# Softmax sums carried as logarithms in the attention of a fused transformer block, with other slots, and two modulation rows sent by way of DRAM

## The chip, the cores and the metric

The kernel runs on one core of a Trainium2 chip. The core has five engines with instruction streams of their own: PE (TensorE, the matrix engine), DVE (VectorE), ACT (ScalarE), POOL (GpSimd) and SP (SyncE, which here only issues transfers). They meet through semaphores alone. Every stream runs in order: an instruction that waits holds up all that stand behind it on its engine. The metric is the device time of one execution in microseconds (us); three runs gave 2748.44, 2750.02 and 2751.23 us, a median of 2750.02 us.

## The reference

One transformer block on 2048 tokens of width 1024, in float32. Six rows of length 1024 (`sa, ca, ga, sb, cb, gb`) come from a small product of a condition vector. Then a normalised and modulated input goes through attention with 32 heads of 32 columns, in four segments of 512 tokens. Inside a segment the softmax is causal; what came before the segment is read through a running sum, the memory:

```python
logits = jnp.einsum("bhqd,bhkd->bhqk", qs, ks) * scale + mask
p = _softmax(logits, axis=-1)
a_dot = jnp.einsum("bhqk,bhkd->bhqd", p, vs)
num = jnp.einsum("bhld,bhde->bhle", pq, M)
den = jnp.einsum("bhld,bhd->bhl", pq, z)[..., None] + 1e-6
a_mem = num / den
o = g * a_mem + (1.0 - g) * a_dot
M = M + jnp.einsum("bhld,bhle->bhde", pk, vs)
...
x = x + ga * _A_ref(h, ...)
h = _layernorm(x, axis=-1) * (1 + cb) + sb
x = x + gb * _B_ref(h, ...)
```

`g` is one number for each head (the sigmoid of `beta`); `_B_ref` is a gated feed-forward of width 3584.

## The kernel before

A factor of every large product is split into a high and a low float32r part, and three products (high·high, high·low, low·high) give the accuracy. The program has four stages: `start` (the six rows, the first segment), 33 steps of attention, the projection with `wo` and the second norm, and the feed-forward (gate and up, then down), which takes the last 1600 us or so.

**The steps of attention.** Step `n` has a group `g` of four heads and a segment `s` (list `steps`, line 1545: first half segments 0 and 1 by turns for each group, second half segments 2 and 3). The work of one (group, segment) is spread over three steps: the products for q, k and v of it are made in step `n-1` (parts K and Q), its scores S, sums A and memory M in step `n`, its values V in step `n+1`. The string `ORDER` (line 1546) is the order in which the parts take turns; each letter runs its generator to the next `yield`. PE's stream is exactly in this order. The streams of DVE, ACT, POOL and SP in this stage are ordered by a scheduler, which lays them out ahead of time by its own costs.

**Scores (S, line 678).** For each block `i` of 128 queries and each head `j`, PE makes a score tile in one of five PSUM banks (`s_ps`). DVE (line 691) adds the mask, copies the negated scores to `sj` and keeps the negated maximum in `mm`; ACT (line 693) takes the exponential of `sj` and keeps its sum in `ll`. When four blocks are done, DVE splits `mm` into a high and a low part `mt`, turns these with four 32x32 transposes into rows `tt` (line 704) and writes them with four `tensor_scalar`s into partitions 96 to 128 of `qs` (line 706). So the product `T` of the values part (line 753), which is the score tile turned round (keys as rows), comes out of PE with the maximum already taken off. Four such `T` products, one for each head, can run only when all four writes of `qs` are done.

**Values (V, line 740).** ACT takes the exponential of `T` into `pt` (line 755), POOL zeroes what the mask forbids (756), and PE multiplies with the values into `po` (762), whose rows are columns of heads and whose columns are queries. The inverse sums are needed in the same orientation: DVE makes `rc = (1-g)/ll` with `omg = 1-g` (710, 711), ACT spreads it to 128 columns `rx` (713), PE turns `rx` with four 128x128 transposes (776, tile `R`), ACT copies the result out (780), DVE multiplies `po` by it (781). For segments after the first, the memory's part `ry` is turned by PE in the same way (tile `Y`) and added by DVE (784).

**K and Q.** A quarter of v or k is six products of 128x512 on PE. The ninth turn of K (line 407) sends k to `ks` and turns it with four transposes (`kT`, line 362), which ACT (`ek`, 364) and DVE (365, 367) make into `pk` for the sums.

**Rows ga and gb.** The columns `modT` hold the six rows as columns. `row_parts` (line 120) makes a row on all partitions of it: DVE puts the columns on two diagonal matrices, PE multiplies them with ones (line 131), ACT copies (132). `gab` is used for `wo` (line 806), `gbb` in the down product.

**Second norm.** `norm_tiles(..., "b")` (line 208) goes through eight tiles of 128 tokens: SP loads a tile `nb` of `x1_d` (line 215) into one of two buffers, DVE takes the statistics, POOL the root, ACT scales it (206), PE turns it (228, `tpb`), ACT shifts it (233, `htb`), SP stores it.

## Time and profile before

| what | value |
|---|---|
| median of three runs | 2750.02 us |
| the profiled execution, its own time | 2750.67 us |
| its span on the core | 2748.8 us |
| busy: PE, DVE, ACT, POOL | 99%, 64%, 47%, 19% of the span |
| PE in the chain that ended last | 91% |

The span is the time from the first instruction of the program to the last; 1.9 us of the execution's own time lie around it. A busy PE row counts from the start of a matrix instruction to its modelled end; since the next one starts before that end, what an instruction takes from PE is read from start to start in the timeline. A wait list names, for each idle time of an engine, the engine whose instruction ended it.

### The profile page before, as it was taken

Reading aid. Unit: us, or ns where it says so; the run is one execution under the profiler, and the core shown is the slowest. Engines: PE = TensorE matmul, PEld = TensorE weight load, DVE = VectorE, ACT = ScalarE, POOL = GpSimd, SP = SyncE. Lnnn points to the kernel's source line nnn. Section 1 sums busy time; section 2 is a strip of 40 time slices with the busy share of each in tenths; the row PEclk is TensorE's granted clock in tenths of the full one; section 3 lists DMA queues with packets and bytes.
Section 4 is the critical chain, followed back from the end, with each engine's and each line's share of the span. In section 5 each row is a group of like instructions: output and inputs, shape, how many; then the busy total and the mean of one; then the engine's idle time right before and its main releaser. Section 6 shows DMA issues by size and latency. Waiting matters only on the chain.

```text
span 2748.8 us, 38576 instructions
## 1 busy us (share of the span) xinstructions
PE 2722.0 (99%) x13346; PEld 2206.8 (80%) x13346; DVE 1755.5 (64%) x3727; ACT 1290.6 (47%) x2858; POOL 515.9 (19%) x970
## 2 busy tenths in 40 slices
PE   8999999999999999999999999999999999999999
PEld 5777877777777777788888888888888888888887
DVE  7566657666666735777777777666777754434552
ACT  6788877677776735333433334223322243332220
POOL 1333333333333421100000000000000003013352
PEclk9999999999999999999999999999999999999999
DMA  8666655665554657656655656433566695544552
GB/s 260 131 139 155 151 116 120 160 140 123 122 114 92 170 187 233 212 209 216 211 210 176 230 205 227 150 123 146 204 249 244 221 311 178 168 140 164 199 193 81
DMA packets 229844, 486.47 MB, mean 177 GB/s; under 512 B 17552, under 2 KB 92560, under 8 KB 229648
## 3 DMA queue, kind: packets, MB, share of 16 engines
q1 hardware_dynamic: 227776, 477.58, 57.5%
q0 software_dynamic: 1728, 6.29, 0.6%
q8 instruction: 105, 1.72, 0.3%
q14 instruction: 91, 0.75, 0.1%
q10 hardware_dynamic: 144, 0.13, 0.0%
HBM read 304.11 MB, written 129.50 MB: 158 GB/s over the span
## 4 chain that ended last, share of the span: by engine, by line
PE 91%; DVE 3%; DMA 3%; ACT 2%; issue 1%; POOL 0%; SPq 0%; DVEq 0%; POOLq 0%; ACTq 0%
PE f L1338 38%; PE d L1509 19%; PE k L320 5%; PE y L821 5%; PE q L320 5%; PE v L320 5%; PE T L753 3%; PE S L689 3%; PE O L762 3%; PE M L669 1%; PE num L727 1%; PE R L776 1%; DMA r<-wv 1%; PE vT L336 1%; ACT sj L693 0%
## 5 line engine op out<-in xcount | busy, mean ns | idle before, releaser
L1338 PE MATMUL f<-A,B 128*128 128x512 f32 x4704 | 1071.8, 390 | 1.2 <-DVE c L1303 0.7
L1338 PEld LDWEIGHTS f<-A,B 128*128 128x128 f32 x4704 | 881.5, 188 | 184.9 <-DVE c L1303 1.1
L1509 PE MATMUL d<-wb,ah 128*128 128x512 f32 x2352 | 534.2, 389 | 0.1
L1509 PEld LDWEIGHTS d<-wb,ah 128*128 128x128 f32 x2352 | 441.5, 188 | 92.4 <-DVE wb L1389 0.5
L691 DVE CUSTOM_DVE_ANT_0 sj<-S,mask 128x384 f32<-128x384 f32 (+3 forms) x512 | 227.2, 487 | 138.3 <-PE S L689 125.3
L693 ACT ACTIVATE sj<-sj,mm 128x384 f32<-128x384 f32 (+3 forms) x512 | 282.1, 558 | 28.4 <-DVE mm L691 26.1
L755 ACT ACTIVATE pt<-T 128x256 f32<-128x256 f32 (+3 forms) x512 | 183.0, 446 | 118.1 <-PE T L753 116.5
L1389 DVE TENSOR_TENSOR ah<-ar,ah 128x1792 fp32r<-128x1792 f32 x56 | 116.2, 2075 | 169.3 <-ACT ah L1388 169.3
L1388 ACT ACTIVATE ah<-ar 128x1792 fp32r<-128x1792 f32 x56 | 95.4, 1703 | 273.8 <-PE d L1509 232.9
L756 POOL TENSOR_SCALAR_AFFINE_SELECT pt<-pt 128x128 f32<-128x128 f32 x512 | 151.4, 315 | 315.1 <-ACT pt L755 308.1
L162 POOL TENSOR_TENSOR w<-r,w 128x256 fp32r<-128x256 f32 x180 | 140.6, 812 | 179.2 <-ACT w L155 160.8
L1305 ACT ACTIVATE g<-g 128x512 f32<-128x512 f32 x56 | 35.4, 633 | 287.0 <-DVE g L1305 287.0
L955 DVE TENSOR_TENSOR B<-t,B 128x512 fp32r<-128x512 f32 x168 | 115.5, 688 | 57.6 <-ACT B L958 57.5
L1414 POOL TENSOR_TENSOR yo<-u,gbb 128x256 f32<-128x256 f32 x32 | 30.1, 972 | 557.2 <-ACT gbb L132 557.2
L958 ACT ACTIVATE B<-t 128x512 fp32r<-128x512 f32 x168 | 105.5, 628 | 58.3 <-PE f L1338 56.0
L821 PE MATMUL y<-wo,hho 128*128 128x512 f32 x384 | 125.9, 393 | 0.0
L1302 ACT ACTIVATE g<-f 128x512 f32<-128x512 f32 x56 | 33.6, 599 | 178.7 <-PE f L1338 178.6
L753 PEld LDWEIGHTS T<-qs,ks 128*128 128x128 f32 x512 | 83.2, 188 | 39.3 <-issue 21.5
L753 PE MATMUL T<-qs,ks 128*128 128x256 f32 (+2 forms) x512 | 111.7, 336 | 3.0 <-DVE ry L735 2.0
L689 PE MATMUL S<-ks,qs 96*128 96x256 f32 (+2 forms) x512 | 110.8, 335 | 2.0 <-DVE mm L691 1.8
L1432 POOL TENSOR_TENSOR xo<-xo,yo 128x256 f32<-128x256 f32 x64 | 71.1, 1141 | 211.8 <-DMA xo<-x_d 196.7
L955 DVE TENSOR_TENSOR B<-rg,B 128x512 fp32r<-128x512 f32 x112 | 77.2, 689 | 51.2 <-ACT B L958 51.1
(255 smaller groups left out, 4314.9 us busy)
## 6 DMA issues: line engine op xcount, KB each, us to landing
ar<-hid_d SPq DMA_DIRECT2D x56, 896.0 KB, 5.2
rg<-wg SPq DMA_DIRECT2D x56, 512.0 KB, 4.7
ru<-wu SPq DMA_DIRECT2D x56, 512.0 KB, 5.5
hid_d<-g SPq DMA_DIRECT2D x56, 512.0 KB, 3.1
sc<-hid_d SPq DMA_DIRECT2D x56, 512.0 KB, 5.7
hid_d<-sc SPq DMA_DIRECT2D x56, 512.0 KB, 2.9
br<-wT_d SPq DMA_DIRECT2D x49, 512.0 KB, 6.1
ks<-kh SPq DMA_DIRECT2D x64, 256.0 KB, 5.6
```

The source lines that it names most:

```text
L162: eng.tensor_sub(w[:, 1, k:k + 256], r[:, k:k + 256], f32(w[:, 0, k:k + 256]))
L320: nc.tensor.matmul(ps, w[:, a], b, start=(kt == 0 and a == 0 and b is hi), stop=(kt == KT - 1 and a == 1))
L689: nc.tensor.matmul(ps[:, :nk], qs[:96, j, i * P:(i + 1) * P], ks[:96, j, :nk], start=True, stop=True)
L691: nc.vector.tensor_tensor_reduce(out=sj[:, :nv], in0=ps[:, :nv], in1=mask[:, L - nv:], scale=-1.0, scalar=3.4e38, op0=ALU.add, op1=ALU.min ...
L693: nc.scalar.activation(sj[:, :nv], sj[:, :nv], AF.Exp, bias=mm[:, j, i:i + 1], scale=-1.0, accum_out=ll[:, i, j:j + 1])
L753: nc.tensor.matmul(ps[:, :nn], ks[:, j, kc * P:(kc + 1) * P], qs[:, j, L - nn:], start=True, stop=True)
L755: nc.scalar.activation(pt, ps[:, nn - n:nn], AF.Exp)
L756: nc.gpsimd.affine_select(pt[:, :P], pt[:, :P], pattern=[[1, P]], compare_op=ALU.is_ge, fill=0.0, base=0, channel_multiplier=-1)
L821: nc.tensor.matmul(ps, b[:, i * P:(i + 1) * P], w[:, a, g % 2], start=(g == 0 and a == 0 and b is hi), stop=(g == G - 1 and a == 1))
L955: eng.tensor_sub(dst[:, k], a[:, k], b[:, k])
L1338: nc.tensor.matmul(ps, B[m, i][:, a, kt * P:(kt + 1) * P], A[p, i, kt][b], start=(start and kt == 0 and a == 0 and b == 0), stop=(kt == 3 ...
L1509: nc.tensor.matmul(ps[t], ops[n][:, x, k, t * P:(t + 1) * P], b[:, y, kk % 2], start=(kk == 0 and x == 0 and y == 0), stop=(kk == 13 and x ...
```

## The change

`ll` becomes its logarithm on ACT and is taken off the (negated) maximum before this is split and turned. So the row that `qs` carries into `T` holds maximum and logarithm of the sum, and the exponential of `T` is the softmax itself. `rc`, `rx`, the four `R` transposes, their copy and the multiplication go; `omg` holds 1-g for each row of `po`, and one DVE instruction makes `po * omg + Y` from it, where `Y` is copied out of PSUM by ACT. Of the four writes of `qs`, those for `i` 1 and 3 go to ACT.

`ORDER` is another one, and the last step has its own (`LAST`, with the old places of T). The first part of V (the four `T` for the first block of keys) stands one turn of K later, the ninth turn of K (with `kT`) stands between the first and the second block of scores and no longer behind the fourth, and the `Y` part ends V. `ga` and `gb` are written to DRAM as columns and read back as a row on all partitions. The loads of `nb` in the second norm are issued by ACT in place of SP. The table of ACT's functions that is loaded at the start is named by the program; it holds both exponential and logarithm.

```diff
+    def row_out(q, c):
+        nc.sync.dma_start(row_d[q * KT:(q + 1) * KT].rearrange("k p -> p k"), modT[:, c:c + KT])
+    def row_in(dst, q):
+        nc.sync.dma_start(dst, row_d[q * KT:(q + 1) * KT].rearrange("k p -> (k p)").unsqueeze(0).to_broadcast([P, D]))
...
         def load(q):
             xs[q] = get(f"n{name}{toks[q]}")
-            nc.sync.dma_start(xs[q], src[toks[q]:toks[q] + P, :])
+            (nc.scalar if name == "b" else nc.sync).dma_start(xs[q], src[toks[q]:toks[q] + P, :])
...
+        nc.scalar.preload_act_table_set("natural_log_exp_and_others")
...
-                                     accum_out=ll[:, i, j:j + 1])
+                                     accum_out=ll[:, j, i:i + 1])
...
+        nc.scalar.activation(ll, ll, AF.Ln)
+        nc.vector.tensor_sub(mm, mm, ll)
         mt = t2("mt" + nm, "mt", bufs=2, dt=F32R, shape=(P, 4, 4, 2))
...
-            nc.vector.tensor_scalar(qs[96:128, :, i * P:(i + 1) * P], tt[96:128].unsqueeze(1).to_broadcast([32, 4, P]),
-                                    seli[96:128, i:i + 1], None, op0=ALU.mult)
-
-        rc = t2("rc" + nm, "rc", bufs=2, shape=(P, 4, 4))
-        nc.vector.reciprocal(rc, ll)
-        nc.vector.tensor_mul(rc, rc, omg[:, 4 * g:4 * g + 4].unsqueeze(1).to_broadcast([P, 4, 4]))
-        rx = t2("rx" + nm, "rx", shape=(P, 4, 4, DH))
-        nc.scalar.activation(rx, rc.unsqueeze(3).to_broadcast([P, 4, 4, DH]), AF.Copy)
+            own, row = qs[96:128, :, i * P:(i + 1) * P], tt[96:128].unsqueeze(1).to_broadcast([32, 4, P])
+            if i in (1, 3, 9):
+                nc.scalar.activation(own, row, AF.Identity, scale=seli[96:128, i:i + 1])
+            else:
+                nc.vector.tensor_scalar(own, row, seli[96:128, i:i + 1], None, op0=ALU.mult)
...
-        rr = tmp_tile("R" + nm)
-        nc.scalar.activation(rr, turned(rx, "R"), AF.Copy)
-        nc.vector.tensor_mul(rr, po, rr)
+        rr = tmp_tile("R" + nm)
+        if s > 0:
+            ps = s_ps("Y" + nm)
             for i in range(4):
+                nc.tensor.transpose(ps[:, i * P:(i + 1) * P], ry[:, i].rearrange("p a b -> p (a b)"), ident)
+            nc.scalar.activation(rr, ps, AF.Copy)
+            nc.vector.scalar_tensor_tensor(rr, po, omg[:, g:g + 1], rr, op0=ALU.mult, op1=ALU.add)
+        else:
+            nc.vector.tensor_scalar_mul(rr, po, omg[:, g:g + 1])
         yield
-        if s > 0:
-            nc.vector.tensor_add(rr, rr, turned(ry, "Y"))
-            yield
...
-                    row_of(gbb, modT[:, 40:48], tmp_tile, "gb")
+                    row_in(gbb, 1)
...
-    ORDER = "K N K K V K V N K K V V K N V K S Q S V V Q M S Q A S K M Q V V"
+    ORDER = "K N K K K V K V N K V V K N V K S Q K S V Q M S Q A S K M Q V"
+    LAST = "K N K K V K V N K K V V N V K S Q S V V Q M S Q A S K M Q V V"
...
-                ga_row = row_parts(gab, modT[:, 16:24], tmp_tile, "ga")
-                todo += [(at, lambda: next(ga_row)) for at in (4, 13, 24)]
+                row_in(gab, 0)
+                todo.append((6, lambda: row_out(1, 40)))
```

The order of the streams at the places that the prediction speaks of, first those behind the last scores of a step (step 6; `0` and `1` in the names are the groups of heads, `33` the last score tile). ACT's stream before, from the last two exponentials of the scores to the first of `T`:

```order
L693 ACTIVATE sj_0_23_3158,ll_0_3033<-sj_0_23_3158,mm_0_3032 128x512
L693 ACTIVATE sj_0_33_3163,ll_0_3033<-sj_0_33_3163,mm_0_3032 128x512
L364 ACTIVATE ek_1_3191<-kT_1_3186 128x512
L373 ACTIVATE qh_1_3202<-q_1_3054 128x512
L376 ACTIVATE eq_1_3205<-q_1_3054 128x512
L713 ACTIVATE rx_0_3181<-rc_0_3178 128x512
L755 ACTIVATE pt_0_00_3261<-T_0_00_3259 128x512
```

The same stretch of ACT's stream now (line numbers are those of the changed file):

```order
L700 ACTIVATE sj_0_23_3120,ll_0_2990<-sj_0_23_3120,mm_0_2989 128x512
L700 ACTIVATE sj_0_33_3125,ll_0_2990<-sj_0_33_3125,mm_0_2989 128x512
L376 ACTIVATE qh_1_3148<-q_1_3011 128x512
L705 ACTIVATE ll_0_2990<-ll_0_2990 128x16
L379 ACTIVATE eq_1_3151<-q_1_3011 128x512
L783 ACTIVATE R_1_3161<-Y_1_3162 128x512
L717 ACTIVATE qs_0_2781<-tt_0_3133,seli 32x4x128 x2
L330 ACTIVATE vr_0_3212<-v_0_3176 128x512
L760 ACTIVATE pt_0_00_3219<-T_0_00_3217 128x512
```

The logarithm (L705) stands behind the last exponential and `qh`; the two writes of `qs` and the copy of `Y` stand ahead of the first exponential of `T`; `ek` and `rx` have left this stretch. DVE's stream in the same stretch before, from the last maximum on:

```order
L691 ISA sj_0_33_3163,mm_0_3032<-S_0_33_3161,mask 128x512
L691 ISA mm_0_3032 128x1
L722 TENSOR_TENSOR mz_1_3492<-Mt_0_3144,blk 128x128
L699 CAST mt_0_3166<-mm_0_3032 128x16
L723 TENSOR_SCALAR mz_1_3492<-sel_100,Mt_0_3144 128x4
L700 TENSOR_TENSOR mt_0_3166<-mm_0_3032,mt_0_3166 128x16
L784 TENSOR_TENSOR R_1_3097<-R_1_3097,Y_1_3215 128x512
L704 STREAM_TRANSPOSE tt_0_3169<-mt_0_3166 32x32 x4
L710 RECIPROCAL rc_0_3178<-ll_0_3033 128x16
L706 TENSOR_SCALAR qs_0_2826<-tt_0_3169,seli 32x4x128 x4
```

And DVE's stream now:

```order
L698 ISA sj_0_33_3125,mm_0_2989<-S_0_33_3123,mask 128x512
L698 ISA mm_0_2989 128x1
L727 TENSOR_TENSOR mz_1_3445<-Mt_0_3106,blk 128x128
L728 TENSOR_SCALAR mz_1_3445<-sel_101,Mt_0_3106 128x4
L706 TENSOR_TENSOR mm_0_2989<-mm_0_2989,ll_0_2990 128x16
L708 CAST mt_0_3130<-mm_0_2989 128x16
L709 TENSOR_TENSOR mt_0_3130<-mm_0_2989,mt_0_3130 128x16
L380 SCALAR_TENSOR_TENSOR ql_1_3149<-q_1_3011,qh_1_3148 128x512
L713 STREAM_TRANSPOSE tt_0_3133<-mt_0_3130 32x32 x4
L384 TENSOR_SCALAR eq_1_3151<-eq_1_3151 128x512
L719 TENSOR_SCALAR qs_0_2781<-tt_0_3133,seli 32x4x128 x2
L386 SCALAR_TENSOR_TENSOR pq_1_3156<-q_1_3011,eq_1_3151 128x512
```

The subtraction (L706) now waits for ACT's logarithm, and `ql` stands between the split and the transposes. The other place is the second norm. SP's stream before, around the load of the seventh tile (`nb_13181`) and of the eighth:

```order
L826 DMA x_d<-xr 128x512
L215 DMA nb_13181<-x_d 128x1024
L234 DMA h_d<-htb_0_13160 128x4x128
L815 DMA xr<-x 128x512
L234 DMA h_d<-htb_1_13171 128x4x128
L215 DMA nb_13244<-x_d 128x1024
```

ACT's stream now, around the same two loads (`nb_12891` and `nb_12954`):

```order
L236 ACTIVATE htb_0_12870<-tpb_0_12869,modT 128x128 x4
L236 ACTIVATE htb_1_12881<-tpb_1_12880,modT 128x128 x4
L218 DMA nb_12891<-x_d 128x1024
L236 ACTIVATE htb_0_12933<-tpb_0_12932,modT 128x128 x4
L236 ACTIVATE htb_1_12944<-tpb_1_12943,modT 128x128 x4
L218 DMA nb_12954<-x_d 128x1024
L209 ACTIVATE nb_12891<-nb_12891,mrb_12976,rsb_12973 128x1024
```

The load of a tile now stands behind the eight shifts `htb` of the tile whose buffer it takes.

## Rows read from the trace of the kernel before

**Rows 1.** The page's first part: the span, and each engine's busy time, share of the span and instructions.

```profile
span 2748.8 us, 38576 instructions
...
PE 2722.0 (99%) x13346; PEld 2206.8 (80%) x13346; DVE 1755.5 (64%) x3727; ACT 1290.6 (47%) x2858; POOL 515.9 (19%) x970
```

**Rows 2.** The list of waits of PE: engine and line, what ended the wait, us in total, times, the longest.

```profile
PE tpb L228 <- ACT nb L206: 3.2, 3, 1.5
PE T L753 <- DVE ry L735: 2.0, 3, 0.9
PE S L689 <- DVE mm L691: 1.8, 4, 0.7
...
PE R L776 <- DVE mm L691: 0.9, 2, 0.5
```

**Rows 3.** PE's groups of instructions, forms kept apart: busy us, mean ns of one | idle us before, and what ended it. One transpose or product in full float32 shows as one or two instructions.

```profile
L776 PE MATMUL R<-ident,rx 128*128 128x128 f32 x128 | 21.0, 286 | 1.0 <-DVE mm L691 0.9
...
L131 PE MATMUL ga<-gadg,ones 128*128 128x512 f32 x4 | 2.1, 618 | 0.0
```

**Rows 4.** PE's timeline in step 15, around the four `R` transposes: start us, length us, engine, line, what.

```profile
525.37 0.86 PE L762 MATMUL O<-pt,vx 128*32 128x256 f32 x16
526.16 0.66 PE L776 MATMUL R<-ident,rx 128*128 128x128 f32 x4
526.57 0.48 PE L320 MATMUL q<-hhh,w 128*128 128x512 f32 x1
526.88 0.40 PE L320 MATMUL q<-hlh,w 128*128 128x512 f32 x1
```

**Rows 5.** PE's timeline around the product for gb, in the down stage.

```profile
2227.87 1.29 PE L1509 MATMUL d<-wb,ah 128*128 128x512 f32 x5
2229.00 1.88 PE L131 MATMUL gb<-gbdg,ones 128*128 128x512 f32 x4
2230.31 1.48 PE L1509 MATMUL d<-wb,ah 128*128 128x512 f32 x4
```

**Rows 6.** Timeline of PE, ACT and DVE behind the last scores of step 6 (the four score products of the last block start at 248.62).

```profile
249.64 0.60 PE L362 MATMUL kT<-ident,kn 128*128 128x128 f32 x4
249.99 0.48 PE L320 MATMUL q<-hha,w 128*128 128x512 f32 x1
...
251.90 0.17 DVE L699 CAST mt<-mm 128x16 fp32r<-128x16 f32 x1
...
252.73 0.19 ACT L693 ACTIVATION_READ_ACCUMULATOR sj<-sj,mm 128x1 f32 x1
252.82 0.58 ACT L364 ACTIVATE ek<-kT 128x512 f32<-128x512 f32 x1
...
252.91 0.86 DVE L704 STREAM_TRANSPOSE tt<-mt 32x32 f32<-32x32 f32 x4
253.06 0.63 PE L320 MATMUL v<-hha,w 128*128 128x512 f32 x2
253.30 0.58 ACT L373 ACTIVATE qh<-q 128x512 fp32r<-128x512 f32 x1
...
254.08 1.69 DVE L706 TENSOR_SCALAR qs<-tt,seli 32x512 fp32r<-32x512 f32 x4
...
254.43 0.62 PE L320 MATMUL v<-hha,w 128*128 128x512 f32 x2
...
256.02 1.08 PE L753 MATMUL T<-qs,ks 128*128 128x512 f32 x4
256.24 0.68 DVE L377 SCALAR_TENSOR_TENSOR ql<-q,qh 128x512 fp32r<-128x512 f32 x1
```

**Rows 7.** Groups of ACT's instructions, forms kept apart, columns as in rows 3: a small exponential, a scaling with two operands of one number per partition, and a load of the function table.

```profile
L497 ACT ACTIVATE x<-x,mra,rsa 128x512 f32<-128x512 f32 x6 | 4.6, 811 | 4.0 <-DVE mra L489 4.0
...
L468 ACT ACT_TABLE_LOAD x1 | 1.3, 1283 | 0.8 <-PEq L1662 0.8
...
L116 ACT ACTIVATE gall<-bb 128x32 f32<-128x32 f32 x1 | 0.2, 237 | 0.0
```

**Rows 8.** PE's timeline in step 16: the memory's product between the last scores and q, and the third and fourth `T`, which waited.

```profile
531.94 1.08 PE L727 MATMUL num<-mz,pq 128*128 128x132 f32 x8
532.77 0.47 PE L320 MATMUL q<-hhh,w 128*128 128x512 f32 x1
...
540.04 0.89 PE L753 MATMUL T<-qs,ks 128*128 128x512 f32 x2 [0.59 <-DVE ry L735]
```

**Rows 9.** Groups of DVE's instructions, forms kept apart, columns as in rows 3.

```profile
L781 DVE TENSOR_TENSOR R<-O,R 128x512 f32<-128x512 f32 x32 | 22.0, 688 | 14.4 <-ACT R L780 14.4
...
L367 DVE SCALAR_TENSOR_TENSOR pk<-kT,ek 128x512 f32<-128x512 f32 x24 | 16.3, 679 | 0.2
...
L365 DVE TENSOR_SCALAR ek<-ek 128x512 f32<-128x512 f32 x24 | 9.7, 406 | 0.4 <-ACT ek L364 0.4
```

**Rows 10.** Timeline in the second norm: the shifts of the fifth tile, the load of the seventh into the same buffer, its statistics and its turn on PE.

```profile
1055.17 2.91 ACT L233 ACTIVATE htb<-tpb,modT 128x128 f32<-128x128 f32 x8 [0.19 <-PE tpb L228]
1055.60 0.33 SPq L215 DMA_DIRECT2D nb<-x_d  x1
...
1060.56 1.29 DVE L193 BATCH_NORM_STATS2 stb<-nb 128x6 f32<-128x512 f32 x2 [6.31 <-DMA nb<-x_d]
...
1065.06 1.09 PE L228 MATMUL tpb<-ident,nb 128*128 128x128 f32 x8 [0.39 <-ACT nb L206]
```

More of the change, by code (lines that the diff above doesn't have):

```diff
@@ L50, in block_kernel @@
     hid_d = [dram.tile([FC // 2 * P, T // 2], F32, name=f"hid{i}_d") for i in range(8)]
+    row_d = dram.tile([2 * KT, P], F32, name="row_d")
     wT_d = dram.tile([FC // 2 * P, 7 * L], F32, name="wT_d")
@@ L109, in block_kernel @@
     gall = cs([P, H], "gall")
-    omg = pa.tile([P, H], F32, name="omg")
+    omg = pa.tile([P, G], F32, name="omg")
     modT = cs([P, 48], "modT")
@@ L133, in row_parts @@
             yield
-    def row_of(*a):
-        for _ in row_parts(*a):
-            pass
+    def row_out(q, c):
+        nc.sync.dma_start(row_d[q * KT:(q + 1) * KT].rearrange("k p -> p k"), modT[:, c:c + KT])
+    def row_in(dst, q):
+        nc.sync.dma_start(dst, row_d[q * KT:(q + 1) * KT].rearrange("k p -> (k p)").unsqueeze(0).to_broadcast([P, D]))
     def mod_load(r, w=None):
@@ L658, in start @@
         sigmoid(gall, bb)
-        nc.vector.tensor_scalar(omg, gall, -1.0, 1.0, op0=ALU.mult, op1=ALU.add)
+        for j in range(4):
+            own = slice(32 * j, 32 * j + 32)
+            nc.vector.tensor_scalar(omg[own], gall.rearrange("p (g j) -> p j g", j=4)[own, j], -1.0, 1.0,
+                                    op0=ALU.mult, op1=ALU.add)
         return norm_seg(1, x1h)
@@ L736, in memory @@
                                         dn[:, 2 * i:2 * i + 2].unsqueeze(3).to_broadcast([P, 2, 4, DH]), op=ALU.mult)
-            SC.setdefault(n, [None, None])[1] = ry
+            SC[n] = ry
         yield
@@ L742, in values @@
         qs, ks, vx, pq = ST.pop(n)
-        rx, ry = SC.pop(n)
+        ry = SC.pop(n, None)
         po = o_ps("O" + nm)
@@ L1596, in block_kernel @@
                          (22, lambda: get(2)), (32, lambda: cut(2)), (26, lambda: get(3)), (35, lambda: cut(3))]
+            if n == 25:
+                todo.append((6, lambda: row_out(0, 16)))
             if rest and n > 0:
@@ L1601, in block_kernel @@
                     todo.append((pos + 23, lambda got=got: mod_col(*got[0], behind=True)))
-            for pos, q in enumerate((ORDER if n else ORDER0).split()):
+            for pos, q in enumerate((ORDER0 if n == 0 else ORDER if n < len(steps) else LAST).split()):
                 for f in [f for at, f in todo if at == pos]:
```

9 lines of the change are left out of this document (2 added, 7 removed).

## The prediction

> **What bounds the kernel now.** The page's first part comes first: PE is busy 2722.0 of 2748.8 us, DVE and ACT 64% and 47% [rows 1]. So the time is PE's work in its fixed order plus some 27 us in which it stands. The list of waits names these: no entry is large, and in the attention and the norm behind it they are a few us each, for PSUM banks that DVE frees (`ry`, `mm`) and for the scaled norm tiles [rows 2]. Therefore a change counts here for what it takes from PE's stream, start to start, and for the waits it makes or ends. Work on DVE and ACT counts only where PE meets its end.
>
> **What leaves PE.** The `R` group has 128 rows, four in each of 32 steps, 21.0 us busy [rows 3]. That busy time overlaps with what follows: in the timeline four transposes start at 526.16 and the next product at 526.57, so a step pays 0.41 us [rows 4]. The product behind them takes 0.31 in place of 0.23 us (526.57 to 526.88), but `O` is full float32 as well and will now stand before it, so I leave this toll in. 32 x 0.41 = **-13.1 us**. The Trainium skill, TensorE: Matmul & The Clock Gate, Part 4, puts a PE transpose at some 275 ns in a kernel; the mean of the row, 286 ns, agrees as a length. By it as a cost the sum would lose 128 x 0.275 = 35 us; start to start the rows show a third of that. The sum goes by the rows.
>
> The product for gb starts at 2229.00, the next group at 2230.31, and this takes 1.48 us for four products, where five took 1.29 ahead of gb and four would take 1.06; so gb costs 1.31 + 0.42 = 1.7 us [rows 5]. The four instructions for ga are as long (618 against 592 ns) [rows 3], the same again: **-3.4 us**. In their place come four small transfers. `gab` is read back a step or more before `wo` needs it and the down product needs `gbb` late, so they lie beside PE's work; if that cover were gone, one landing, 5 us at most like the load in [rows 10], would be paid once.
>
> **What the new slots cost PE.** `kT` in the old place stood next to `num`, another full float32 product, in the 15 odd steps that have both; the toll of 0.09 us on the way back to split products was paid once (the first q behind `num` is 0.47 us long, as behind `R`, 0.48) [rows 4, 8]. In the new place it stands between q and scores and pays for itself: 15 x 0.09 = **+1.4 us**.
>
> **Waits that end.** `T` waited 2.0 us for banks that `ry` frees, the longest at 540.04 [rows 2, 8]. DVE now does `ry` before the subtraction, inside the time in which it waits for ACT's logarithm, some 3 us earlier. `R` waited 0.9 us for `mm` [rows 2]. Both go: **-2.9 us**. Bounds 0 and -2.9, as the wait for the banks could come back in front of another product.
>
> **The chain to T.** This is the place to watch, since a step's `T` needs all four writes of `qs`. In step 6 before, the split starts at 251.90 without ACT, the transposes end at 253.77, the writes at 255.77, and `T` starts at 256.02: 0.25 us of room [rows 6]. Now:
> - ACT's last sum is read by 252.92. `ek` has gone ahead, so `qh` starts at 252.82 and the logarithm 0.48 later, at 253.30. It has 16 columns; the nearest row is an exponential of 32, 0.24 us [rows 7]: 253.54.
> - DVE subtracts, casts, subtracts: three dependent instructions, 0.2 us each as from the cast at 251.90 on: 254.15. `ql` holds the transposes up by 0.6 of its 0.68 us: they run from 254.75 to 255.6 [rows 6].
> - Then two writes on DVE behind `eq` (0.4, then half of 1.69): 256.85; beside them two on ACT. No row has an activation with one per-partition operand from 512 columns; with two it takes 0.81 us [rows 7], with none 0.58 (`qh`) [rows 6]. I take 0.7, overlapping by 0.1: 255.65 + 1.3 = 256.95.
> - `T` itself comes later: less `kT` (249.64 to 249.99), plus a quarter of k, six products, 253.06 to 254.43 = 1.37 us [rows 6]. 256.02 - 0.35 - 0.1 + 1.37 = 256.95.
>
> So it is even: chain and PE arrive together. In steps where `num` lies between scores and `T` too, PE comes 0.8 us later [rows 8], and there is room. That leaves the 7 even steps of the first half (2 to 14). Bounds: from nothing (writes of 0.58) to 7 x 0.5 = 3.5 us (writes of 0.81, 0.2 more for the handing over). I take **+1.0 us**, which includes the exponentials of `T`, which have one turn of K less before the product with the values.
>
> **DVE among the scores.** `ek` and `pk` (0.41 + 0.68 us) move in between the score maxima in 23 steps, the `R` multiplication (0.69) moves out: +0.4 us [rows 9]. It costs PE only where DVE is behind; `S` waited 1.8 us in four places before [rows 2]. Bounds -1.8 (the waits vanish) and 8 x 0.4 = 3.2 us (all odd steps of the second half): **+0.8 us**.
>
> **Second norm.** This speaks against the change. Before, the seventh tile's load was issued at 1055.60, as soon as PE had turned the fifth, and PE still stood 0.39 us for it [rows 10]. ACT's stream now has that load behind the eight shifts of the fifth tile, which end at 1058.08: 2.5 us later. The load to statistics takes 5.0 us (1055.60 to 1060.56), the rest of the chain is as long, so PE would stand 2.9 us, +2.5. The third tile's load comes later by the same means but the fourth's earlier, which about cancels. ACT's queue holds no other transfers; were the landing a us or two faster for that, the loss would go, and at best the 3.2 us of `tpb` waits with it [rows 2]. The Trainium skill, DMA: Bandwidth & Descriptors, Rules for kernel authors, says that spreading transfers over issuing engines buys no bandwidth, only issue time. By that the landing stays and the term is +2.5; no row here can show it. Bounds -3.2 and +4 (both places): **+1.8 us**.
>
> **Sum**, against the profiled execution of 2750.67 us: -13.1 - 3.4 + 1.4 - 2.9 + 1.0 + 0.8 + 1.8 = -14.4, so 2736.3; the median of the runs is 0.65 lower. I say **2736 us**. The bounds added up reach from -22 to about -4; not all fall on one side, so its own range is 2730 to 2743.
>
> **Rivals.**
> - *The chain decides in many steps* (2743 us). If the handing over between ACT and DVE costs 0.2 us at each of its four crossings and the writes take 0.81, `qs` is 1.0 us later; 7 steps pay 1 and some 16 pay 0.2: +10 on the +1 of the sum, partly given back in the next scores, so +7. For it: DVE and ACT streams are fixed ahead and `ql` already stands in the way. Against it: most steps have `num` or `Y` and so room [rows 8].
> - *Scores bound by DVE* (2744 us). If DVE, not PE, paces the stretch with the scores, the time of `R`, which lay there, comes back as waits for `mm`: of 13.1 us some 8 are lost. Against it: DVE's idle time there outweighs PE's waits of 1.8 us, and `kT` fills the slot.
> - *Slower than before* (2757 us). ACT is in order, and each step puts `w` splits and `ek` among the exponentials. If ACT ends the scores late, the logarithm, the subtraction, the transposes and the writes come late with it, and PE stands at `T` in every step. The gain is eaten from 14.4 / 32 = 0.45 us of mean wait per step on; with the room of 0 to 0.8 us that is a chain about 1.0 to 1.3 us longer than mine in all steps. At 1.1 us of mean wait: 2736 + 32 x 0.65 = 2757. Against it: ACT is idle half the time, and in step 6 the last exponential was done at 252.92, 1 us behind the cast of the maxima [rows 6].
> - *A table load at each switch* between exponential and logarithm: two per step, 64 x 1.28 us = 82 us on ACT [rows 7], of which the logarithm's, 1.28, lies in the chain and the next delays the exponentials of `T`: 32 x 1.3 at least, 2778 us. The Trainium skill, ScalarE: Activation LUTs, Table sets, has one set with both functions, and ACT's new stream has no second load in the attention; hardly likely.
>
> **How the numbers follow.** Forecast 0.72; the chain 0.12; scores 0.08; slower 0.05; table loads 0.01; a gain above 21 us (all waits vanish) 0.02. What a measurement can tell from no change is 0.2%, 5.5 us: faster means under 2744.5. The forecast is faster but for its last hundredth, of the chain and the scores cases two in three: 0.71 + 0.14 + 0.02 = 0.87; slower 0.05 + 0.01 = 0.06; the same 0.07. The range of 8 in 10 takes in the bounds and most of the first two rivals: 2728 to 2744.
>
> **What would show it.** No `R` rows on PE, 128 fewer transposes, no ga and gb: PE's busy time (2722.0) down by some 15 us; the 25 us of the groups' own rows are not the gain. A wait of `T` for `qs` (DVE or ACT) in the first half's even steps of about 0.1 us each; entries of 0.5 us in all steps would show the chain. `T` <- `ry` gone. `S` <- `mm` near 2 us; 10 would show the scores case. `tpb` <- `nb` near 5 us with the seventh tile the longest. One table load before the feed-forward. The forecast is wrong if PE's stream shrinks as told and its idle time grows by more than 8 us.

## The result and the profile after

The changed kernel is slower: a median of 2771.93 us over six runs (2769.7 to 2773.5) against 2750.12 us of the kernel before on the same chip, a ratio of 1.0078 with a 95% interval of 1.0066 to 1.0089. The forecast was 2736 us with a range to 2744. The profiled execution took 2769.8 us, its span 2768.1, 19.3 us more than before.

The page's first part after:

```profile
span 2768.1 us, 38291 instructions
...
PE 2721.0 (98%) x13210; PEld 2195.8 (79%) x13210; DVE 1726.2 (62%) x3606; ACT 1315.0 (48%) x2910; POOL 518.5 (19%) x970
```

The 136 instructions that should leave PE have left it (13346 before [rows 1]). DVE has less to do, ACT little more. But PE's busy time is only 1 us lower, and its idle time (span less busy time) grew from 26.8 to 47.1 us. The list of PE's waits after (us in total, times, the longest) answers to [rows 2]:

```profile
PE T L758 <- DVE qs L719: 10.0, 18, 1.9
PE sc L132 <- DVE scdg L126: 7.4, 1, 7.4
PE O L767 <- POOL pt L761: 7.1, 8, 1.0
PE M L676 <- DVE mm L698: 4.7, 1, 4.7
PE S L696 <- DVE mm L698: 1.8, 3, 0.7
PE tpb L231 <- ACT nb L209: 1.8, 3, 1.2
```

`T <- ry` and `R <- mm` are gone, as forecast. Three new entries stand in their place: `T` for `qs`, `O` for POOL's selects, `M` for a maximum. The `sc` entry is the start's and was there before.

A wait in this list counts only full idleness. What a part takes from PE's stream shows when PE's timeline is added up from each instruction's start to the next one's, by what the instruction makes. A wait then falls to the product ahead of it: one of `T` to `v`, one inside `O` to `O`. These sums run from the first score of step 1 to that of step 31, in us, worked out from the timelines of the profiled executions; the other columns are experiments told below, "best" the last of them. Small parts are left out.

| part | before | after | old slots | splits moved | no logarithm | best |
|---|---|---|---|---|---|---|
| R | 12.3 | 0 | 0 | 0 | 0 | 0 |
| O | 74.8 | 94.5 | 81.0 | 79.0 | 99.9 | 75.9 |
| v | 160.7 | 173.9 | 230.9 | 167.2 | 160.5 | 163.3 |
| S | 88.9 | 94.1 | 89.6 | 97.9 | 93.8 | 100.5 |
| q | 171.2 | 176.2 | 172.9 | 171.3 | 171.3 | 171.1 |
| T | 87.0 | 82.3 | 94.2 | 82.3 | 80.6 | 81.8 |
| kT | 10.5 | 7.8 | 10.5 | 7.8 | 7.8 | 7.8 |
| k | 162.7 | 161.0 | 161.7 | 168.4 | 161.4 | 161.8 |
| all parts | 850.3 | 872.2 | 927.1 | 855.5 | 861.9 | 843.1 |

So the expected gain is there: `R` gives 12.3 us, `T` 4.7, `kT` 2.6. Four places take more than it: `O` 19.7, `v` ahead of `T` 13.3, `S` 5.2, `q` 4.9 (this is the wait of `M`).

**T waits.** The timeline after in step 10, behind the last scores (PE's products of v run without a gap; the last one starts at 376.61):

```profile
373.29 0.20 ACT L705 ACTIVATE ll<-ll 128x16 f32<-128x16 f32 x1
...
373.52 0.18 DVE L706 TENSOR_TENSOR mm<-mm,ll 128x16 f32<-128x16 f32 x1 [1.41 <-ACT ll L705]
...
374.12 0.69 DVE L380 SCALAR_TENSOR_TENSOR ql<-q,qh 128x512 fp32r<-128x512 f32 x1
...
374.34 1.05 ACT L158 ACTIVATE w<-r 128x1024 fp32r<-128x1024 f32 x1
...
374.84 0.86 DVE L713 STREAM_TRANSPOSE tt<-mt 32x32 f32<-32x32 f32 x4
...
375.48 3.36 POOL L165 TENSOR_TENSOR w<-r,w 128x256 fp32r<-128x256 f32 x4 [7.22 <-ACT w L158]
...
375.73 0.76 DVE L384 TENSOR_SCALAR eq<-eq 128x512 f32<-128x512 f32 x1
375.74 1.33 ACT L717 ACTIVATE qs<-tt,seli 32x512 fp32r<-32x512 f32 x2 [0.34 <-DVE tt L713]
...
376.52 1.72 DVE L719 TENSOR_SCALAR qs<-tt,seli 32x512 fp32r<-32x512 f32 x2
...
378.39 0.93 PE L758 MATMUL T<-qs,ks 128*128 128x512 f32 x3 [1.39 <-DVE qs L719]
```

DVE stands 1.41 us for ACT's logarithm. Then, beside POOL's subtraction for the low part of `w`, the minimum takes 0.76 us and the two writes of `qs` 0.86 us each. One line of the trace's groups, minimum/median/maximum in ns, for DVE's writes after, and the same for the kernel before:

```profile
L719 DVE TENSOR_SCALAR qs<-tt,seli x64: 479/486/1483, 77.5 to 985.6; 32x512 fp32r<-32x512 f32 x64
```

```profile
L706 DVE TENSOR_SCALAR qs<-tt,seli x128: 479/481/489, 75.2 to 961.3; 32x512 fp32r<-32x512 f32 x128
```

All 128 writes before took 0.48 us. After, the 36 that lie clear of POOL still do, and the 28 that lie beside its subtractions (of `w` and `wo`, in one place of a loaded `h`) take 0.85 us and more. The Trainium skill, SBUF — State Buffer, section Who interferes with whom, says that a `tensor_scalar` of VectorE in a mode with two ports and an instruction of GpSimd exclude each other for a whole instruction. The trace agrees as far as it goes: 0.37 to 0.51 us more a write (but for the one of 1483 ns), less than one piece of POOL's subtraction (four take 3.36 us here). And the one that begins first is not held up: before, the last of the four writes lay over the beginning of POOL's subtraction in eight steps, by 0.29 to 0.40 us, and kept its 0.48. The kernel before was at this edge. In step 12, which is clear of POOL, DVE's last write ends 16.97 us behind the first score now and 15.14 us before: the chain has become 1.8 us later, and in other steps that puts the writes beside POOL.

**O waits.** The timeline after in step 9, from the first exponentials of the second `T` to the product with the values:

```profile
349.57 1.06 ACT L158 ACTIVATE w<-r 128x1024 fp32r<-128x1024 f32 x1
...
350.53 1.61 ACT L760 ACTIVATE pt<-T 128x384 f32<-128x384 f32 x4
...
350.71 1.43 POOL L165 TENSOR_TENSOR w<-r,w 128x256 fp32r<-128x256 f32 x2 [0.81 <-ACT w L158]
...
352.33 0.74 POOL L165 TENSOR_TENSOR w<-r,w 128x256 fp32r<-128x256 f32 x1
...
352.51 1.65 DVE L149 CUSTOM_DVE_ANT_0 wm<-wm,scb 128x1024 f32<-128x1024 f32 x1
353.01 1.29 POOL L761 TENSOR_SCALAR_AFFINE_SELECT pt<-pt 128x128 f32<-128x128 f32 x1
...
354.36 0.83 PE L767 MATMUL O<-pt,vx 128*32 128x384 f32 x2 [0.99 <-POOL pt L761]
```

ACT's split of q's weights stands ahead of the second set of exponentials, and POOL's four pieces of its low part stand among the selects; one select takes 1.29 us in place of 0.29. That select does not lie beside the split but beside an instruction of DVE for a column of `modT` (L149), and ends 0.14 us behind it; in all the six steps named below it is so. No select of the kernel before begins beside such an instruction, and those that begin ahead of one keep their 0.29 (three before, three after). `O` is 2.99 us longer than before in each of steps 9, 11, 21, 23, 25 and 27; about 1.0 us of it is this meeting, and only the rest the pieces of the split themselves. The cost does not show as waits alone: before, the products of the four heads start 0.01 us apart and run side by side; now they start one by one as their selects end. Of the 19.7 us at `O` about 13 stand in PE's busy time and 7 in its idle time.

**M waits.** The transfers after around 870 to 885 us: the line of busy tenths and the one of GB/s in 40 slices, and the packets; then SP's issues, the multiplication that waits, and PE:

```profile
DMA  0296758998899999909939979999981934577999
GB/s 0 33 240 153 218 164 317 459 382 306 285 190 309 363 295 175 44 0 33 60 11 33 33 33 33 27 22 60 27 71 55 60 44 93 191 197 191 202 251 186
DMA packets 1791, 2.19 MB, mean 146 GB/s; under 512 B 1114, under 2 KB 1114, under 8 KB 1790
```

```profile
870.62 0.42 SPq L137 DMA_DIRECT2D row_d<-modT  x1
871.10 0.57 SPq L98 DMA_DIRECT2D ro<-wo  x1
...
884.87 1.23 DVE L808 TENSOR_TENSOR ro<-ro,gab 128x1024 f32<-128x1024 f32 x1 [5.94 <-DMA ro<-wo]
...
886.49 2.10 PE L676 MATMUL M<-vx,pk 128*128 128x130 f32 x8 [4.72 <-DVE mm L698]
```

The write of row gb is 8 columns by 128 partitions, 1024 packets of 4 bytes. For 6 us (16 slices from 876 on) the DMA engines are mostly busy and move 0 to 71 GB/s. The small packets themselves stand mostly at 874 to 876; from 876 to 882 some 30 packets of 4 KB take 1.7 us each in the median, where those at 870 to 874 took 0.16. A load of `wo` issued behind it at 871.10 is there at 884.87 only, 13.8 us later. DVE, in order, waits for it with the maxima behind, ACT and PE with it.

### The profile page after: what moved, and what is told of

Same layout as the page of the kernel before. It is cut to its first block, busy times and chain, and to the rows that moved or that the text cites. A ratio compares the mean times of both kernels' runs of the same rounds, so it can differ in the third digit from the quotient of the medians.

```text
span 2768.1 us, 38291 instructions
## 1 busy us (share of the span) xinstructions
PE 2721.0 (98%) x13210; PEld 2195.8 (79%) x13210; DVE 1726.2 (62%) x3606; ACT 1315.0 (48%) x2910; POOL 518.5 (19%) x970
## 4 chain that ended last, share of the span: by engine, by line
PE 59%; DVE 1%; DMA 0%; ACT 0%; issue 0%; DVEq 0%; SPq 0%; ACTq 0%
PE f L1340 37%; PE d L1511 19%; PE y L823 2%; PE tpb L1188 0%; DMA ar<-hid_d 0%; DVE wb L1391 0%; DVE sc L1323 0%; DVE A L957 0%; DMA hid_d<-sc 0%; ACT wb L1390 0%; DVE s L1044 0%; DVE B L957 0%; ACT ah L1390 0%; DVE g L1307 0%; ACT L1304 0%
## 5 line engine op out<-in xcount | busy, mean ns | idle before, releaser
L1302 ACT ACTIVATE c<-f 128x512 f32<-128x512 f32 x56 | 33.5, 599 | 159.2 <-PE f L1340 159.2
```

## The experiments

Each ran beside the kernel before on the same chip; a ratio is to that. Where the times of two experiments are compared, it is by their medians; the kernel before had 2749.9 to 2750.3 us beside all of them. What was written before the run stands ahead of its measurement.

**Old slots.** `ORDER` is that of the kernel before in all steps.

> The changed kernel with the old ORDER in all steps (T one turn of K earlier, kT behind the fourth block of scores, two turns for V's end). In the changed kernel the products O take 19.7 us more than before between steps 1 and 31, the v products ahead of T 13.3 us more (T waits for qs). Theory (the split of w by POOL stands in front of the selects of the second T only because T was moved; the chain of the logarithm has no room): O gives back about 18 us, the waits of T for qs grow by 0.7 to 1.3 us in each of 30 steps, 20 to 40 us: 2772 - 18 + 30 = about 2784 us. Rival (the slots alone cost the time, the chain has room): O gives back 18 us, the scores 5, T waits no more than now: about 2750 us.

Measured: 2824.52 us, ratio 1.0275 (1.0256 to 1.0294). The waits:

```profile
PE T L758 <- DVE qs L719: 59.2, 28, 3.3
```

`O` gives back 13.5 us, `v` grows by 57. The direction is that of the theory, the size 40 us beyond it; part of that is the clock (last section). With the logarithm in the chain the old slots cost 53 us more than the new ones, so the later `T` was needed, and it took most of the time at `O` (13.5 of 19.7 us). The run moves `T` and `kT` at once; `kT` alone is told below.

**Row gb late.** 

```diff
+                if n == 0:
+                    row_out(1, 40)
                 if n == 2:
                     row_in(gbb, 1)
...
-                todo.append((6, lambda: row_out(1, 40)))
```

> The changed kernel with the write of row gb to DRAM moved out of step 29 into the down stage, two tiles ahead of its reading. Theory (this write is 1024 packets of 4 bytes which hold all the queues for some 6 us, so that a load of wo behind it lands after 13.7 us and DVE, which waits for it, holds up the maxima: 4.7 us of wait of M for mm, and 5.0 us more on the q products): the wait M <- DVE mm goes, 2772 - 5 = about 2767 us. Rival (the multiplication with gab stands badly in DVE's order whatever the transfers do): the wait stays, 2772 us.

Measured: 2762.09 us, ratio 1.0045 (1.0028 to 1.0062), 9.8 us under the changed kernel where 5 were expected. The wait of `M` is gone. `q` gives back 5.1 us, and `M`, `S` and `num` behind it 0.9, 0.9 and 0.8, which is the clock again (last section); the profiled execution's span is 7.7 us less.

**Splits moved.** The numbers are the place in `ORDER`, 0 to fetch and 1 to split, and 0, 1, 2 for the weights of q, v, k; `behind` pins the split in ACT's order behind what was issued ahead of it.

```diff
-[(4, 0, 1), (8, 0, 2), (15, 1, 1), (20, 1, 2), (24, 0, 0), (31, 1, 0)]
+[(4, 0, 1), (8, 0, 2), (15, 1, 1), (29, 1, 2), (24, 0, 0), (41, 1, 0)]
...
-            W[g][i] = split_w(raws[i], wsp_tile(f"w{i}_{half}_{g}"), behind=False)
+            W[g][i] = split_w(raws[i], wsp_tile(f"w{i}_{half}_{g}"), behind=i != 1)
```

> The changed kernel with two of the three splits of w pinned elsewhere in ACT's order: that of k's weights behind the writes of qs, that of q's weights behind the exponentials of the second T. Theory (POOL's part of the split slows DVE's writes of qs from 0.48 to 0.96 us and stands in front of the selects): DVE's qs 0.48 us in nearly all steps, O gives back some 17 of 19.7 us, the waits of T for qs fall from 10.0 to some 4 us: 2772 - 17 - 6 = about 2749 us. Rival (the chain with the logarithm and T's one turn less are too long by themselves): waits stay within 3 us of now, about 2770 us.

Measured: 2755.17 us, ratio 1.0019 (1.0009 to 1.0028). The waits of PE:

```profile
PE T L758 <- DVE qs L719: 5.0, 11, 1.6
PE vT L339 <- ACT pt L760: 3.8, 3, 1.3
...
PE O L767 <- POOL pt L761: 2.7, 5, 1.0
PE k L323 <- ACT w L158: 2.3, 1, 2.3
```

57 of 64 writes of `qs` are back at 0.48 us, `O` gives back 15.5 us, `v` 6.7. So two thirds of what `O` and `v` lost (22.2 of 33.0 us) hang on where two splits stand beside the later chain. `k` takes 7.4 us more than in the changed kernel, with a wait for a pinned split among it, and `S` 3.8, in steps 13, 15, 29 and 30; this takes some of the gain back. `q` falls too, since here no load of `wo` stands behind the write of row gb.

**kT back.** One K turn less in `ORDER` of steps 1 to 29, so that `kT` stands behind the fourth scores.

> The changed kernel with kT back behind the fourth block of scores (steps 1 to 29), all else as changed. Theory (ek and pk on DVE among the maxima hold up the scores by 0.43 us in each of the first 14 steps): S gives back some 5 us, and T comes 0.35 us later behind the chain, 2 to 4 us of its waits go: about 2764 us. Rival (the scores' 0.43 us is the turn from float32 transposes to scores, paid wherever kT stands): about 2771 us.

Measured: 2782.33 us, ratio 1.0119 (1.0104 to 1.0134): 10 us slower than the changed kernel, against both theories. `S` gives back 7.0 us, as expected. But ACT's `ek` is then ahead of the logarithm, and DVE's minimum of `ek` and `pk` (0.43 and 0.69 us) stand in the chain to `T`, whose waits for `qs` grow from 10.0 to 17.5 us.

**Low part on DVE.** Row gb late, q's split moved as above; of k's weights DVE makes the low part, meant to stand behind its writes of `qs`.

```diff
+        def low(i):
+            w = W[g][i]
+            tc.keep_in_program_order(nc.vector.tensor_sub(w[:, 1], raws[i], f32(w[:, 0])))
```

> The changed kernel with the write of row gb late (as in the run with that edit alone), q's weights split behind the exponentials of the second T (as in the run with the moved splits), and of k's weights the low part taken by DVE behind its writes of qs in place of POOL, the high part where the scheduler puts it. Theory (POOL beside the writes of qs, POOL ahead of the selects and the small packets are what ate the gain of the missing R): all three go without the new waits of k and vT that the moved split brought (3.8 + 2.3 us): 2755 - 6 - 2 = about 2747 us, the same as before or a little faster. Rival (the chain with the logarithm is at its limit in most steps, any DVE work near it costs): T's waits for qs stay at 5 us or grow, 2755 us.

Measured: 2752.46 us, ratio 1.0010 (1.0001 to 1.0019). `O` is down to 77.6 us; `v` stays at 172.5, and `S` rises to 100.4, in steps 13, 15, 19 and 29. The low part stands behind the writes of `qs` in the first half alone. In the even steps 16 to 28 the scheduler put it into the chain itself, between the subtraction of the logarithm and the split of the maximum, and each of them loses 0.7 us at `v`; step 20:

```profile
651.29 0.18 DVE L714 TENSOR_TENSOR mm<-mm,ll 128x16 f32<-128x16 f32 x1 [0.24 <-ACT ll L713]
651.38 1.22 DVE L321 TENSOR_TENSOR w<-r,w 128x1024 fp32r<-128x1024 f32 x1
652.51 0.17 DVE L716 CAST mt<-mm 128x16 fp32r<-128x16 f32 x1
```

The time is between the two expectations; `T` still waits 9.1 us for `qs`, as the rival has it, and part of that is this place.

**Minima on POOL.** As the run before, `nc.gpsimd` for the minima of `ek` and `eq`.

> As the run with the low part on DVE, and the two minima of ek and eq go from DVE to POOL. Theory (0.43 us a step of the scores in the first half are DVE's ek and pk among the maxima, and eq's minimum stands ahead of the writes of qs): 0.4 us less DVE at both places, S gives back 2 to 5 us, T's waits 2 us: about 2742 us. Rival (POOL takes over 1 us for it and DVE's pk and pq, which wait for it, hold up the maxima and the writes longer than now): slower, 2755 us or more.

Measured: 2760.91 us, ratio 1.0040 (1.0027 to 1.0052). The rival came true, 8.5 us over the run before: a minimum takes POOL 1.49 us, `pq` waits for it and stands ahead of the writes of `qs`; `v` grows to 182.6 us.

**All of qs on DVE.** As the run with the low part on DVE, without ACT's writes.

> As the run with the low part on DVE, but all four writes of qs on DVE, as in the kernel before. Theory (the chain to T decides in most steps): the last write ends 4 x 0.42 = 1.7 us behind the transposes in place of 1.33 us (ACT's two) or eq's 0.4 + 0.9 us; 0.4 us in some 25 steps: 10 us slower than that run, about 2757 us. Rival (T is reached with room in most steps): within 2 us of that run.

Measured: 2799.07 us, ratio 1.0179 (1.0165 to 1.0193), 46.6 us slower than that run where 10 were expected. The waits:

```profile
PE T L766 <- DVE qs L727: 30.1, 25, 2.0
PE kT L373 <- ACT kn L360: 10.6, 4, 2.8
...
PE S L704 <- DVE mm L706: 7.4, 5, 4.0
```

`T` waits for DVE's writes in 25 places. So the chain to `T` decides in most steps once DVE has all four writes, and the later chain needs ACT's two. Of the 43.8 us that the profiled span is longer than in that run, 30.5 are idle time of PE and 13.3 busy time (last section).

**Rows and norm alone.** The kernel before with rows ga and gb by way of DRAM (gb late) and the loads of `nb` by ACT.

> The kernel before with only the two rows ga and gb by way of DRAM (gb written late, in the down stage) and the loads of nb in the second norm issued by ACT; softmax sums, slots and qs as before. Theory (in the changed kernel ga and gb gave 1.0 + 1.4 us, the norm about 0.7): 2750.3 - 3 = about 2747 us. Rival by the prediction's terms (ga and gb -3.4, norm +1.8): 2748.7 us with tpb waiting about 5 us for nb, in place of 3.2.

Measured: 2750.17 us, ratio 1.0002 (0.9993 to 1.0011); `tpb` waits 2.9 us for `nb`. The interval reaches from -1.9 to +3.0 us, so the -3 expected for the whole did not come, and the -1.6 of the prediction's terms cannot be told from 0. But the run has a new wait that the two parts do not contain:

```profile
PE T L756 <- DVE qs L709: 2.2, 1, 2.2
```

It stands in step 10, where three of the four writes of `qs` lie beside POOL and take 0.94 to 0.96 us; the step is 2.5 us longer than before. The down stage is 1.8 us shorter without the product for gb. So the parts gave about what was expected, and another order of the streams took it back, as far as this one profiled execution shows.

**No logarithm.**

```diff
-        nc.scalar.activation(ll, ll, AF.Ln)
-        nc.vector.tensor_sub(mm, mm, ll)
```

> The changed kernel without the logarithm and its subtraction: the rows of T are not divided by their sums, all else as changed. Theory (DVE stands some 1.4 us in each step for ACT's last sums and the logarithm, and that makes the chain to T late): the split starts 1.6 us earlier, the waits of T for qs fall from 10.0 to about 1 us, the v products ahead of T give back some 10 of 13.3 us, O stays 19.7 us too long: about 2761 us. Rival (POOL beside the writes of qs makes T wait): at most a third of it goes, about 2768 us.

Measured: 2759.24 us, ratio 1.0035 (1.0022 to 1.0049), 12.7 us under the changed kernel. The largest entry of the waits that is new beside the kernel before:

```profile
PE O L765 <- POOL pt L759: 9.1, 13, 1.1
```

No entry of `T` for `qs` is left, and `v` is back at 160.5 us, 13.4 less. All 64 writes of `qs` take 0.48 to 0.52 us:

```profile
L717 DVE TENSOR_SCALAR qs<-tt,seli x64: 479/484/517, 74.5 to 972.2; 32x512 fp32r<-32x512 f32 x64
```

In step 12 the last one of DVE ends 13.98 us behind the first score, 3.0 us earlier than with the logarithm (1.6 were expected), and so before POOL begins. So it is the wait for ACT that makes the chain late, and being late puts it beside POOL. `O` stays 25 us too long (three more steps have it): that cost is another one. The time alone would mislead, since the edit moves other things too: the wait of `M` is not there (`q` gives back 4.9 us), and `O` takes 5.4 more.

**ql behind.** `ql`, the minimum of `eq` and `pq` are held behind DVE's last write of `qs`.

> The changed kernel with ql, the minimum of eq and pq on DVE held behind DVE's two writes of qs. Theory (ql 0.69 and eq 0.42 to 0.84 us stand in the chain to T): the waits of T for qs fall from 10.0 to 2 or 3 us, O unchanged: about 2764 us. Rival (the chain hangs on ACT's two writes, 1.33 us behind the transposes, and on POOL): the waits fall by less than 3 us, 2769 us or more.

Measured: 2770.31 us, ratio 1.0075 (1.0062 to 1.0089). The waits of `T` for `qs` fall to 4.3 us and `v` gives back 8.7, as the theory has it; but the time is the rival's, since `T` takes 4.9 and `O` 2.6 more (`pq` and `ql` now hold banks of `q` longer: `k`, behind `T`, waits 4.7 us for `pq`, from step 17 on).

**By halves**, and **by halves with ql behind.** Row gb late, q's split moved; k's weights as in the run with the low part on DVE in the first half, as in the run with the moved splits in the second. The second run adds the edit of `ql`.

> Row gb late; q's weights split behind the exponentials of the second T; k's weights in the first half as in the run with the low part on DVE, in the second half as in the run with the moved splits, each the better there by its steps. Theory (costs of the places add up): steps 1 to 12 as the kernel before, steps 16 to 28 some 0.8 us each below it, the steps with loads of h and o (13 to 15, 29, 30) some 7 us above it: about 2746 us. Rival (the gain of one place comes back as a wait at the next): 2752 us.

> As the run by halves, and ql, eq's minimum and pq held behind DVE's writes of qs. Theory (chain to T short by 1 us): T's waits of 0.3 to 0.7 us in the even steps go too: 2742 us, faster than the kernel before by 0.3%. Rival (pq and ql late hold up the DMA of qs or the maxima of the next step): no better than the run by halves, 2746 to 2750 us.

Measured: 2747.43 us, ratio 0.9988 (0.9979 to 0.9997), and 2745.03 us, ratio 0.9983 (0.9975 to 0.9992). The first is what was expected, 2746: the costs of the places do add up. The second was to reach 2742. Its 2.4 us under the first are not clear of the spread (2745.1 to 2749.5 and 2741.4 to 2750.2 us over eleven runs each); in the profiled executions `v` gives back 4.3 us and `O` 2.4, `M`, `q` and `S` take 4.8, and no wait of `k` for `pq` is left.

**M ahead**, alone and in the run before; the letter A moves in `ORDER` behind the K that makes `kT`.

> The changed kernel with the product M (part A) moved ahead, directly behind kT, in place of between the third and the fourth block of scores. Theory (kT holds one of the five banks of the scores until DVE has made pk, and pk waits for M, which still reads the one buffer of pk: 0.43 us of the scores in each of the first 14 steps): S gives back 5 us, M stands beside kT: about 2767 us. Rival (ek and pk simply take DVE's time among the maxima): S stays 0.43 us long in these steps, 2771 us or more.

> The run by halves with ql behind, and M ahead as in the run before. Theory: 2745 - 5 = about 2740 us, 0.35% under the kernel before. Rival (S's 0.43 us come back as a wait for mm, as DVE is the limit among the scores): 2745 us.

Measured: 2780.24 us, ratio 1.0111 (1.0098 to 1.0125), and 2756.54 us, ratio 1.0022 (1.0013 to 1.0031). Both are slower, by 8.3 and 11.5 us, where 5 less were expected of each. The theory of the single buffer of `pk` falls: in the first run `S` gives back 1.6 us in steps 1 to 12, where the changed kernel loses 6.0, and waits from step 10 on until `M` has been copied out of its bank (3.0 us); `O` grows by 4.1 us and `T` by 3.1. In the second `O` grows by 8.3.

**Casts of h and o on ACT**, in the run before (with `late=True`).

> As the run before, and in steps 14, 15 and 30 the high parts of the loaded h and o are made by ACT in place of DVE. Theory (in steps 13 to 15, 29 and 30 DVE with these casts is late with maxima, selects and sums: 8 us over the kernel before): 3 to 4 us less than that run, about 2737 us. Rival (ACT, in the chain itself, becomes late): slower than that run by 2 us or more.

Measured: 2753.09 us, ratio 1.0012 (1.0003 to 1.0021), 3.5 us under the run before, the difference that was expected, from a higher start. Steps 13 to 15 give 5.5 us; the products of the projection (`y`) take 3.3 of it back.

**The best.** The run by halves with `ql` behind, M in its place, and the casts of `h` alone on ACT.

> The run by halves with ql behind (M in its place), and in steps 14 and 15 the high parts of the loaded h made by ACT in place of DVE. Theory (DVE's casts there make maxima and sums late: steps 13 to 15 stand 6.7 us above the kernel before in that run): 4 to 5.6 us go, as they did with M ahead: about 2740 us, 0.35% under the kernel before. Rival (ACT, which carries the chain, becomes late instead, or the time comes back at the next step): 2744 us or more.

Measured: 2740.97 us, ratio 0.9966 (0.9952 to 0.9979), 9 us faster than the kernel before. The waits of PE:

```profile
PE S L708 <- DVE mm L710: 6.4, 6, 2.3
PE tpb L231 <- ACT nb L209: 4.0, 3, 1.9
PE T L770 <- DVE qs L731: 1.9, 2, 1.6
PE O L779 <- POOL pt L773: 1.3, 3, 0.6
```

The page's first part:

```profile
PE 2707.4 (99%) x13210; PEld 2192.5 (80%) x13210; DVE 1716.1 (63%) x3597; ACT 1322.1 (48%) x2926; POOL 488.8 (18%) x942
```

With `O` repaired PE's busy time is 14.6 us under that of the kernel before, the 15 us that the prediction named as a sign. This is the changed kernel with the splits, the write of one row, three DVE instructions a step and a few casts put elsewhere. It still pays 11.6 us at `S` against the kernel before. None of these moves was tried on the kernel before, so how much of the 9 us belongs to the change and how much to the moves is not shown.

## Why the prediction was wrong

- *What leaves PE.* Right. 0.41 us a step, 12.3 in 30 steps. For ga and gb 3.4 were right too: ga's own products took 1.0 us and those behind them 0.8 more (0.52 in place of 0.12, 0.63 in place of 0.23), gb 1.31 and 0.41, and the down stage is 1.65 us shorter. The sign named for it, busy time down by 15 us, failed all the same: `O` and `S` took up 13.0 and 4.3 us of busy time. The prediction's own sign of being wrong, idle time up by more than 8 us, came: 20.3.
- *Waits that end.* Right: neither `T <- ry` nor `R <- mm` is left; `T` is 4.7 us shorter, more than the 2.0 taken. (The longest of the old waits is one of 0.85 us at 511.78, not the one at 540.04.)
- *kT.* Wrong sign: `kT` and `num` take 2.6 and 0.7 us less; +1.4 was forecast. The toll of a switch back to split products is not paid by q any more but, 0.08 us, by the scores behind `kT`.
- *The chain to T.* **This is the step that failed**: "I take +1.0 us, which includes the exponentials of `T`, which have one turn of K less before the product with the values." It measured 13.3 us at `v` and 19.7 at `O`. Its working held to 0.1 us as far as the transposes: moved to step 10 by the start of the logarithm (373.29 against 253.30), they were to end at 375.59 and ended at 375.70. From there it priced the rest by step 6 [rows 6], where POOL stands still: `eq` 0.42 and writes of 0.42, where beside POOL they took 0.76 and 0.86. In the even steps of the first half that are clear of POOL (2, 4, 6, 12, 14) `v` lost 0.3 to 0.4 us, inside the bound of 0.5; beside POOL's split steps 8 and 10 lost 1.6 each, and the odd steps 1 to 7, which were thought to have room, 0.3. With the splits moved steps 3, 5 and 7 lose nothing and all seven even steps 2.7 us together, inside the bound of 3.5. And for the exponentials the working asked only how many turns of K PE has, and not what stands ahead of them on ACT and POOL: a split of `w` of 1.06 us, four pieces of 0.74 us, and a select held to 1.29 us beside DVE's L149. The queue of the engine between was never counted.
- *DVE among the scores.* Right mechanism, mis-sized, wrong place: +0.8 us taken, 5.2 measured, beyond the bound of 3.2; 0.41 to 0.48 us in each of steps 2 to 14 (1.18 in step 1), and 0.15 or less in the odd steps 17 to 27 of the second half, the half that the bound was worked out from. With `kT` back it goes altogether. Whether DVE's time or the bank of `kT` is the limit stays open: with M ahead both changed at once.
- *Rows ga and gb.* "they lie beside PE's work; if that cover were gone, one landing, 5 us at most". The cover was gone for another transfer: the price was 7.7 us of the span, by a load queued behind the small packets. The Trainium skill, DMA: Bandwidth & Descriptors, Specifications, gives 512 bytes as the least transfer for line rate. The trace agrees in the rate, 0 to 71 GB/s behind packets of 4 bytes. The rule was not weighed.
- *Second norm.* The term of +1.8 did not come: `tpb` waits 1.8 us in place of 3.2. Over the other kernels run here, all with these loads on ACT, it waits 0.7 to 4.0 us, so no part of the change can be read from it.
- *The rivals.* "The chain decides in many steps" (+7 us) named what `T` does and was half the size; the runs without the logarithm and with all writes on DVE show it. "Slower than before" (ACT with `w` splits among the exponentials) had the right sign by a wrong mechanism: in step 10 the logarithm begins 3.55 us ahead of the end of PE's products of v, against 3.65 in the working, so it is not the exponentials of the scores that come late, but the split behind them that hurts. No second table load came.
- *The sum.* The lower bounds of the terms add up to -23.0 us, not -22. The upper end, -4, was passed by 26 us: `O` and `v` took 33, where the term for the chain had a bound of 3.5.

## What to carry to other kernels

A chain that gets longer by a wait between engines must be laid over every engine's queue at its new time, in the steps where that queue is full: take the durations from a step with the split beside it, not from a clear one. When a product is moved later towards its consumer, list what the engines between (here ACT and POOL) have queued in that gap before counting PE's turns. A transfer's cost is its packets and what is queued behind it, not its bytes.

## What the runs showed of the hardware

A wait costs PE more than its length. Around the wait of 4.72 us the windows of the changed kernel read (columns: us; PE, PEld, DVE, ACT, POOL busy with counts; granted TensorE clock; DMA share; GB/s):

```profile
881.00:886.40 5.40, 0.77 (x4) 0.30 (x2) 1.53 (x4) 0.00 (x0) 0.89 (x2) 0.88 0.83 146
886.40:888.00 1.60, 1.51 (x7) 1.51 (x8) 1.60 (x9) 1.53 (x5) 0.00 (x0) 0.50 0.87 193
888.00:890.00 2.00, 2.00 (x7) 1.71 (x7) 1.47 (x6) 1.56 (x7) 0.00 (x0) 0.50 0.28 91
...
892.00:895.00 3.00, 3.00 (x17) 2.46 (x16) 2.21 (x11) 2.35 (x8) 0.00 (x0) 1.00 0.01 3
```

While PE stood these 4.72 us, its clock fell: it was granted at 0.50, the level of 1.2 GHz, until about 892, and `M`, `S` and `num` took 2.5 us more. The run with row gb late, without that wait, has these 2.5 us back. In the run with all of `qs` on DVE the clock fell behind a wait of 1.91 us too; the products behind it then start 0.43 us apart (537.97 to 538.40) in place of 0.23, and the clock of 536 to 540 us reads 0.61:

```profile
535.53 1.20 PE L766 MATMUL T<-qs,ks 128*128 128x512 f32 x4 [1.91 <-DVE qs L727]
...
537.97 0.63 PE L331 MATMUL k<-hlh,w 128*128 128x512 f32 x1
538.40 0.63 PE L331 MATMUL k<-hhh,w 128*128 128x512 f32 x1
```

The length of one wait does not tell by itself: behind one of 1.87 us at 466.4 in the changed kernel and one of 2.77 at 814.8 in that run the clock stayed at full speed.

In windows of 4 us from 240 to 960 us, what the clock lacks of full speed adds up to some 12 us in that run and some 19 in the run with the old slots, against 3.4 in the changed kernel and none in the kernel before. PE's busy time tells the same: 13.3 us more than in the run with the low part on DVE, and 8.6 more with the old slots than in the changed kernel. This is part of why both came out well beyond their expectations; the rest is longer waits.
